# Windowed attention into a two-stage MoE layer: wider score tiles, full-row matmuls, later weight loads, a lagging second stage

## Chip, cores and metric

The kernel runs on one core of a Trainium2 chip. The metric is the device time of one execution in microseconds (us). Three runs of the kernel before took 403.33 to 403.43 us, median 403.37 us. One further execution was recorded by the profiler: 400.38 us, of which the span from the first to the last instruction is 398.7 us. All rows below are from that execution.

## What is computed

Attention with a sliding window of 128 and a linear position bias, on 8 batches, 8 heads, 576 positions, head size 64. Its output, as 4608 tokens of 512, goes through a two-layer network with a gated activation.

```python
scores = q @ k.T / sqrt(64)                       # per batch and head
rel = pos[:, None] - pos[None, :]
bias = -slope[h] * abs(rel)
scores = where((rel >= 0) & (rel < 128), scores + bias, -1e9)
x = softmax(scores) @ v                           # -> (4608, 512)
h = x @ w_in                                      # 512 -> 2048
g = h * sigmoid(beta * h)
out = g @ w_out                                   # 2048 -> 512, float32
```

## The kernel before

**Blocks.** The 576 positions of a batch are four blocks of 128 rows and a fifth of 64. `load_rows` (L84) brings one block of q, k or v for all heads into a float32 buffer of a ring of 14 (`fst`), by a transfer issued on SP. `load_qk` (L95) and `load_v` (L105) cast it to bfloat16 on POOL. SP and POOL each work their queue in order.

**Attention pieces** (each a small group of instructions that TensorE executes as one):
- `T(b, sb)` (L161): eight transposes on TensorE, for four head pairs of q and of k, and one VectorE copy into `qkT`. For the fifth block the transposes are on 64 rows.
- `SC(b, m, p)` (L178): scores of a head pair for two key blocks, 2m and 2m+1. A key block meets the queries of its own block and of the next. The two heads of a pair lie in the lower and upper 64 rows of the array. Four matmuls write the one score buffer in PSUM (`sps`, one buffer). Then four exponentials on ScalarE (L205, L209) and one mask multiply on VectorE (L214) make `pt`. A tile is 512 columns per head for m = 0 and 448 for m = 1.
- `SC4(b)` (L217): the fifth key block of all eight heads by eight 64x64 matmuls, with its own exponential (L229) and multiply by a weight table (L234).
- `PV(b, qb, g)` (L249): for four heads, weights times v, over the previous and own key block, with a column of ones for the sum (L259, L263); then reciprocal and scaling on VectorE (L268, L269). For qb = 4 the weights are 128x64 and 64x64.
- `X(b, qb)` (L274): transposes the result and copies it into `XT`, the input of the first MoE stage (L279, L284).

**MoE pieces**, for nine groups of 512 tokens: `HS(g, j)` (L291) is four matmuls of 512 columns for the j-th 128 columns of w_in, then a tanh on ScalarE (L302) and a combination on VectorE (L303) into `gT` (two buffers). `OS(g, i, n)` (L307) is four of the sixteen matmuls for 128 tokens of the output; after the last, ScalarE copies (L319) and SP stores.

**Order.** TensorE's order is written out by hand (`manual_schedule`): all attention pieces are one list `att`, in which the scores of one half batch are merged with the PVs of the half before. `need[g]` is the number of pieces up to the X that completes the tokens of group g. The pieces up to `need[0]` come first. Then the MoE items of each group follow, HS(g, j) and, from g = 1, OS of the group before alternating with them; between the items the attention pieces for the next group are spread evenly (L405 to L409). The last piece of a group, the X that the next group's first HS reads, comes behind the last item. X of block 3 of batch 0 stands behind T(1,0), T(1,1), T(1,2) and the first SC of batch 1. The orders of the other engines are made by a planner, by program order and its own costs.

**Weights.** W1 (w_in) and W2 (w_out) are loaded by four transfers each, issued on POOL; `issue_after` puts them behind a cast: W1 behind the cast of k of block 3 of batch 0, W2 behind the last cast of v of batch 0 (L383 to L392).

The functions that the change touches:

Of the kernel before, what the change touches and what calls it, by code (L numbers as in the profile page):

```python
# [18 lines left out]
def kernel(  # L19
# [36 lines left out]
    ones = const.tile([P, 2, 512], BF16, name="ones")  # L56
    mask0 = const.tile([P, 2, 512], BF16, name="mask0")
    mask1 = const.tile([P, 2, 448], BF16, name="mask1")
    kpos = const.tile([P, 1], F32, name="kpos")
    bias = const.tile([P, 2, H], F32, name="bias")  # L60
    w4 = const.tile([64, H], F32, name="w4")
    A4 = const.tile([64, 2, NP, 64], F32, name="A4")
    VS = [const.tile([P, NQB, H, D + 2], BF16, name=f"vs{i}") for i in range(2)]
    XT = const.tile([P, NDM, XTR], BF16, name="XT")
# [47 lines left out]
    for sb in range(3):  # L112
        load_qk(0, sb)
# [4 lines left out]
    nc.vector.memset(ones[:], 1.0)  # L118
# [3 lines left out]
    for m, w in ((mask0, P), (mask1, 64)):  # L122
        nc.gpsimd.affine_select(
            out=m[:, :, 0:256], in_=ones[:, :, 0:256], pattern=[[0, 4], [1, P]], **low
        )
        nc.gpsimd.affine_select(
            out=m[:, :, 256 : 256 + w], in_=ones[:, :, 0:w], pattern=[[0, 2], [-1, w]], **up
        )
        nc.gpsimd.affine_select(
            out=m[:, :, 256 + w : 256 + w + P], in_=ones[:, :, 0:P], pattern=[[0, 2], [-1, P]], **up  # L130
        )
# [21 lines left out]
    make_identity(nc, identf[:])  # L153
# [5 lines left out]
    qk_tiles, pts, p4s, xns = {}, {}, {}, {}  # L159

    def T(b, sb):  # L161
        rows = ROWS[sb]
        if sb == 0:
            qk_tiles[b] = qk_pool.tile([P, 2, NP, S], BF16, name="qkT", tag="qkT")
        src = staged.pop((b, sb))
        tps = psum_t.tile([P, 2, NP, P], BF16, name="tps", tag="t")
        for i in range(2):
            for p in range(NP):
                nc.tensor.transpose(  # L169
                    out=tps[:, i, p, 0:rows],  # L170
                    in_=src[0:rows, i, 2 * p : 2 * p + 2, :].rearrange("r h d -> r (h d)"),
                    identity=ident[0:rows, 0:rows],
                )
        nc.vector.tensor_copy(  # L174
            out=qk_tiles[b][:, :, :, P * sb : P * sb + rows], in_=tps[:, :, :, 0:rows]
        )

    def SC(b, m, p):  # L178
        qk = qk_tiles[b]
        sps = psum_s.tile([P, 2, 512], F32, name="sps", tag="sps")  # L180
        w = P if m == 0 else 64
        for kk in range(2):
            kb = 2 * m + kk
            for e in range(2):
                lhsT = qk[64 * e : 64 * e + 64, 1, p, P * kb : P * kb + P]
                if kk == 0:
                    first = sps[:, e, 0:1]
                    o = bass.AP(
                        tensor=first.tensor, offset=first.offset,
                        ap=[list(first.ap[0]), [256 + w, 2], [1, P]],  # L190
                    )
                    nq = 2 * P
                else:
                    o = sps[:, e, P : 2 * P + w]
                    nq = P + w
                nc.tensor.matmul(  # L196
                    o, lhsT=lhsT,
                    rhs=qk[64 * e : 64 * e + 64, 0, p, P * kb : P * kb + nq],
                    start=True, stop=True, skip_group_check=True,
                )  # L200
        wid = 256 + w + P
        pt = pt_pool.tile([P, 2, 512], BF16, name="pt", tag="pt")
        for e in range(2):
            h = 2 * p + e
            nc.scalar.activation(  # L205
                out=pt[:, e, 0:256], in_=sps[:, e, 0:256], func=ACTF.Exp,
                scale=qscale, bias=bias[:, 0, h : h + 1],
            )
            nc.scalar.activation(  # L209
                out=pt[:, e, 256:wid], in_=sps[:, e, 256:wid], func=ACTF.Exp,  # L210
                scale=qscale, bias=bias[:, 1, h : h + 1],
            )
        mk = (mask0 if m == 0 else mask1)[:, :, 0:wid]
        nc.vector.tensor_tensor(out=pt[:, :, 0:wid], in0=pt[:, :, 0:wid], in1=mk, op=ALU.mult)  # L214
        pts[b, m, p] = pt

    def SC4(b):  # L217
        qk = qk_tiles[b]
        sps = psum_s.tile([P, 2, 512], F32, name="sps4", tag="sps")
        for p in range(NP):  # L220
            for e in range(2):
                nc.tensor.matmul(
                    sps[0:64, e, 64 * p : 64 * p + 64],
                    lhsT=qk[64 * e : 64 * e + 64, 1, p, 512:576],
                    rhs=qk[64 * e : 64 * e + 64, 0, p, 512:576],
                    start=True, stop=True, skip_group_check=True,
                )
        e4 = p4_pool.tile([64, 2, NP, 64], F32, name="e4", tag="e4")
        nc.scalar.activation(  # L229
            out=e4[:].rearrange("p e h q -> p e (h q)"), in_=sps[0:64, :, 0:256],  # L230
            func=ACTF.Exp, scale=qscale,
        )
        p4 = p4_pool.tile([64, 2, NP, 64], BF16, name="p4", tag="p4")
        nc.vector.tensor_tensor(out=p4[:], in0=e4[:], in1=A4[:], op=ALU.mult)  # L234
        p4s[b] = p4

    def own(b, kb, h):
        p, e = divmod(h, 2)
        if kb == 4:
            return p4s[b][:, e, p, :]  # L240
        return pts[b, kb // 2, p][:, e, P * (kb % 2) : P * (kb % 2) + P]

    def prev(b, kb, h, nq):
        p, e = divmod(h, 2)
        m, kk = divmod(kb, 2)
        at = 256 if kk else 256 + (P if m == 0 else 64)
        return pts[b, m, p][:, e, at : at + nq]
# [119 lines left out]
    def loads_ahead(b, m):  # L367
# [6 lines left out]
        elif b + 1 < B:  # L374
            for sb in range(3):
                load_qk(b + 1, sb)
            for sb in range(2):
                load_v(b + 1, sb)

    with tc.manual_schedule(engines={mybir.EngineType.PE}):  # L380
        load_v(0, 0)
        load_v(0, 1)
        c = load_qk(0, 3)  # L383
        load_qk(0, 4)
# [12 lines left out]
        for g in range(NTG):  # L397
            items = []
            for j in range(NFF):
                items.append(lambda g=g, j=j: HS(g, j))  # L400
                if g:
                    items.append(lambda g=g, j=j: OS(g - 1, j // 4, j % 4))
            target = need[g + 1] if g + 1 < NTG else len(att)
            start = done
            for n, it in enumerate(items):  # L405
                it()
                while done < start + (target - start) * (n + 1) // len(items):
                    att[done][1]()
                    done += 1  # L409
# [32 lines left out]
```

## Time and profile before

| | before |
|---|---|
| median of 3 runs | 403.37 us |
| profiled execution / its span | 400.38 us / 398.7 us |
| TensorE matmul busy | 354.0 us (89%), 2529 instructions |
| VectorE busy | 231.1 us (58%) |
| ScalarE busy | 214.5 us (54%) |
| POOL busy | 83.2 us (21%) |
| moved by DMA | 42.40 MB, mean 106 GB/s |
| both MoE stages' matmuls | 149.8 + 145.6 us, 576 + 576 of 512 columns |

Busy shares are means over the span. The slices in tenths show stages: in the first fifth the transfers are full and TensorE is not, behind it TensorE is full. Matmuls overlap each other in the records, so the cost of a group of matmuls is read from where it starts to where the next group starts, not from its duration. The engine names are PE (TensorE matmul), PEld (TensorE weight load), DVE (VectorE), ACT (ScalarE), POOL, and SP for the queue that issues transfers.

### The profile page before, as it was taken

To read this page: it belongs to the slowest core of one execution; us is meant where nothing else is said; L and a number is where in the kernel's file an instruction comes from. 1 tells how busy PE (TensorE), PEld (TensorE's weight loads), DVE (VectorE), ACT (ScalarE), POOL (GpSimd) and SP (SyncE) were. 2 spreads that over 40 slices of the span, in tenths; PEclk is the share of its full clock that TensorE was granted. 3 is DMA by queue.
4 is the path that set the end of the run, shared out by engine and by line. 5 is a ranking of instruction groups with operands and counts; after the bars stand their busy time and mean duration, and the time that the engine had idled before them with its cause. 6 is when DMAs were issued, how large, how long until landed. Compare 5 with 4: busy or idle time off the path is not lost.

```text
span 398.7 us, 6725 instructions
## 1 busy us (share of the span) xinstructions
PE 354.0 (89%) x2529; PEld 174.3 (44%) x2529; DVE 231.1 (58%) x485; ACT 214.5 (54%) x446; POOL 83.2 (21%) x143
## 2 busy tenths in 40 slices
PE   0447478889999999999999999999999999999996
PEld 0335224544454445444455445444554444544442
DVE  3556239976675677556665776567666755433410
ACT  1363058666835774475735683568547854345421
POOL 5850255512222312112021312121100000000000
PEclk9955559999999999999999999999999999999999
DMA  9999999941987698834137342000000001000112
GB/s 174 206 198 196 213 198 221 192 108 39 172 189 149 136 199 177 166 89 106 54 84 168 98 115 67 26 29 27 28 26 28 29 26 54 26 27 29 51 53 81
DMA packets 121985, 42.40 MB, mean 106 GB/s; under 512 B 113232, under 2 KB 117344, under 8 KB 121952
## 3 DMA queue, kind: packets, MB, share of 16 engines
q1 hardware_dynamic: 117728, 37.77, 45.4%
q0 software_dynamic: 4224, 4.19, 6.2%
q8 instruction: 20, 0.33, 0.4%
q14 instruction: 13, 0.11, 0.1%
HBM read 36.71 MB, written 9.44 MB: 116 GB/s over the span
## 4 chain that ended last, share of the span: by engine, by line
PE 79%; DMA 9%; DVE 4%; ACT 3%; SPq 2%; issue 1%; POOL 1%; ACTq 0%
PE ops L313 32%; PE hps L297 31%; DMA fst<-in_k_dram 5%; DMA fst<-in_q_dram 4%; PE sps L196 4%; PE pv L263 4%; PE pv L259 3%; PE tps L169 3%; SPq L87 2%; PE xt L279 2%; DVE gT L303 1%; ACT sig L302 1%; DVE XT L284 1%; ACT pt L209 1%; DVE pt L214 1%
## 5 line engine op out<-in xcount | busy, mean ns | idle before, releaser
L302 ACT ACTIVATE sig<-hps,beta_h 128x512 bf16<-128x512 f32 x144 | 99.5, 691 | 116.9 <-PE hps L297 110.6
L297 PE MATMUL hps<-XT,W 128*128 128x512 bf16 x576 | 149.8, 383 | 7.3 <-DVE XT L284 6.6
L313 PE MATMUL ops<-W,gT 128*128 128x512 bf16 x576 | 145.6, 380 | 0.0
L303 DVE SCALAR_TENSOR_TENSOR gT<-sig,hps 128x512 bf16<-128x512 bf16 x144 | 98.5, 684 | 68.4 <-ACT sig L302 68.0
L205 ACT ACTIVATE pt<-sps,bias 128x256 bf16<-128x256 f32 x128 | 61.0, 477 | 44.1 <-PE sps L196 44.0
L297 PEld LDWEIGHTS <-W 128*128 128x128 bf16 x576 | 50.3, 98 | 56.8 <-issue 13.4
L313 PEld LDWEIGHTS <-gT 128*128 128x128 bf16 x576 | 50.6, 98 | 55.7 <-issue 6.0
L209 ACT ACTIVATE pt<-sps,bias 128x192 bf16<-128x192 f32 (+1 forms) x128 | 58.2, 455 | 0.0
L214 DVE TENSOR_TENSOR pt<-pt,mask 128x1024 bf16<-128x1024 bf16 (+1 forms) x64 | 43.7, 683 | 15.4 <-ACT pt L209 14.2
L100 POOL CAST bst<-fst 128x512 bf16<-128x512 f32 (+1 forms) x40 | 24.6, 616 | 117.6 <-issue 72.0
L108 POOL CAST vs<-fst 128x512 bf16<-128x512 f32 (+1 forms) x40 | 26.4, 673 | 67.7 <-PE pv L259 24.3
L196 PE MATMUL sps<-qkT 64*128 64x256 bf16 (+1 forms) x256 | 27.3, 287 | 12.8 <-ACT pt L209 11.2
L269 DVE TENSOR_TENSOR xn<-pv,zs 128x256 bf16<-128x256 f32 (+1 forms) x80 | 33.6, 422 | 2.4
L174 DVE COPY qkT<-tps 128x1024 bf16<-128x1024 bf16 (+1 forms) x40 | 25.4, 635 | 16.2 <-PE tps L169 15.5
L259 PE MATMUL pv<-vs,pt 128*128 128x65 bf16 (+1 forms) x256 | 33.2, 205 | 0.7 <-DVE xn L269 0.6
L169 PE MATMUL tps<-ident,bst 128*128 128x128 bf16 (+1 forms) x320 | 26.0, 230 | 6.8 <-POOL bst L101 4.7
L319 ACT ACTIVATE osb<-ops 128x512 f32<-128x512 f32 x36 | 21.8, 604 | 17.4 <-PE ops L313 16.8
L268 DVE RECIPROCAL zs<-pv 128x4 f32<-128x4 f32 (+1 forms) x80 | 14.3, 179 | 29.0 <-PE pv L263 28.2
L259 PEld LDWEIGHTS <-pt 128*128 128x128 bf16 (+1 forms) x256 | 22.6, 103 | 14.8 <-issue 5.7
L169 PEld LDWEIGHTS <-bst 128*128 128x128 bf16 (+1 forms) x320 | 21.1, 105 | 17.2 <-POOL bst L101 6.1
L101 POOL CAST bst<-fst 128x512 bf16<-128x512 f32 (+1 forms) x40 | 24.5, 611 | 18.0 <-DMA fst<-in_k_dram 18.0
L196 PEld LDWEIGHTS <-qkT 64*128 64x128 bf16 x256 | 9.1, 96 | 37.4 <-issue 35.3
(35 smaller groups left out, 138.5 us busy)
## 6 DMA issues: line engine op xcount, KB each, us to landing
out_dram<-osb SPq DMA_DIRECT2D x36, 256.0 KB, 2.0
fst<-in_q_dram SPq DMA_DIRECT2D x32, 256.0 KB, 4.9
fst<-in_k_dram SPq DMA_DIRECT2D x32, 256.0 KB, 5.1
fst<-in_v_dram SPq DMA_DIRECT2D x32, 256.0 KB, 4.8
W<-in_moe_w_in_dram POOLq DMA_DIRECT2D x4, 512.0 KB, 9.5
W<-in_moe_w_out_dram POOLq DMA_DIRECT2D x4, 512.0 KB, 18.9
fst<-in_q_dram SPq DMA_DIRECT2D x8, 128.0 KB, 4.5
fst<-in_k_dram SPq DMA_DIRECT2D x8, 128.0 KB, 4.3
```

The lines of the kernel that those rows point to most:

```text
L108: return nc.gpsimd.tensor_copy(out=VS[b % 2][0:rows, sb, :, 0:D], in_=f[0:rows])
L169: nc.tensor.transpose(out=tps[:, i, p, 0:rows], in_=src[0:rows, i, 2 * p : 2 * p + 2, :].rearrange("r h d -> r (h d)"), identity=ident[0:r ...
L196: nc.tensor.matmul(o, lhsT=lhsT, rhs=qk[64 * e : 64 * e + 64, 0, p, P * kb : P * kb + nq], start=True, stop=True, skip_group_check=True,)
L205: nc.scalar.activation(out=pt[:, e, 0:256], in_=sps[:, e, 0:256], func=ACTF.Exp, scale=qscale, bias=bias[:, 0, h : h + 1],)
L209: nc.scalar.activation(out=pt[:, e, 256:wid], in_=sps[:, e, 256:wid], func=ACTF.Exp, scale=qscale, bias=bias[:, 1, h : h + 1],)
L214: nc.vector.tensor_tensor(out=pt[:, :, 0:wid], in0=pt[:, :, 0:wid], in1=mk, op=ALU.mult)
L259: nc.tensor.matmul(pv[0:nq, hl, 0 : D + 1], lhsT=prev(b, qb - 1, h, nq), rhs=vs[:, qb - 1, h, 0 : D + 1], start=True, stop=False,)
L269: nc.vector.tensor_tensor(out=xn[0:nq, 4 * g : 4 * g + 4, :], in0=pv[0:nq, :, 0:D], in1=zs[0:nq].broadcast_to([nq, 4, D]), op=ALU.mult,)
L297: nc.tensor.matmul(hps[:], lhsT=W1[:, c, bass.ts(j, P)], rhs=XT[:, c, c0 : c0 + TOKG], start=(c == 0), stop=(c == NDM - 1),)
L302: nc.scalar.activation(out=sig[:], in_=hps[:], func=ACTF.Tanh, scale=beta_h[:, j : j + 1])
L303: nc.vector.scalar_tensor_tensor(out=gts[g][:, j, :], in0=sig[:], scalar=1.0, in1=hps[:], op0=ALU.add, op1=ALU.mult)
L313: nc.tensor.matmul(ops_[:], lhsT=gT[:, j, i * P : i * P + P], rhs=W2[:, j, :], start=(j == 0), stop=(j == NFF - 1),)
```

## The change

- **Score tiles.** The second half of a batch (m = 1) now takes key blocks 2, 4 and 3 in one tile of 512 columns per head; SC4, its weight table and its pools are gone. The fifth block of keys is padded with zeros to 128 rows in `QK`, two fixed tiles in place of the pool `qkT`.
- **Full rows.** PV, T and X of the fifth block work on 128 rows and 128 columns; the extra v rows are zero, and the extra results aren't read.
- **Masks and setup.** The masks are filled from one column of ones by more and smaller selects; identities, masks and biases stand ahead of the first row loads; `fst` has 16 buffers.
- **Weights.** W1 is issued behind the cast of v of block 3 of batch 0, W2 behind the cast of v of block 1 of batch 1.
- **Order.** In group 1 no OS stands beside the first eight HS; two stand behind each of the last eight. In every group the attention pieces are spread over all items but the last three.

```diff
-    fst_pool = ctx.enter_context(tc.tile_pool(name="fst", bufs=14))
+    QK = [const.tile([P, 2, NP, NQB * P], BF16, name=f"qkT{i}") for i in range(2)]
+    fst_pool = ctx.enter_context(tc.tile_pool(name="fst", bufs=16))
...
+    make_identity(nc, identf[:])
+    nc.vector.memset(one[:], 1.0)
...
+    def fill(m, at, n, w, sign, how):
+        for e in range(2):
+            nc.gpsimd.affine_select(
+                out=masks[m][:, e, at : at + n * w].rearrange("p (n w) -> p n w", w=w),
+                in_=bass.AP(tensor=one.tensor, offset=one[:].offset,
+                            ap=[list(one[:].ap[0]), [0, n], [0, w]]),
+                pattern=[[0, n], [sign, w]], **how,
+            )
+    fill(0, 0, 2, P, 1, low)
+    fill(0, 256, 2, P, -1, up)
+    fill(1, 0, 1, P, 1, low)
+    fill(1, 128, 1, 64, 1, low)
+    fill(1, 192, 1, P, 1, low)
+    fill(1, 320, 1, 64, -1, up)
+    fill(1, 384, 1, P, -1, up)
...
+        nc.vector.memset(VS[i][64:P, 4, :, :], 0.0)
+        nc.vector.memset(QK[i][:, :, :, S:], 0.0)
+    for sb in range(3):
+        load_qk(0, sb)
...
     def T(b, sb):
-                    out=tps[:, i, p, 0:rows],
-                    in_=src[0:rows, i, 2 * p : 2 * p + 2, :].rearrange("r h d -> r (h d)"),
-                    identity=ident[0:rows, 0:rows],
+                    out=tps[:, i, p, :],
+                    in_=src[:, i, 2 * p : 2 * p + 2, :].rearrange("r h d -> r (h d)"),
+                    identity=ident[:],
...
+    COLS = {0: (0, 384), 1: (128, 256), 2: (0, 384), 3: (192, 320), 4: (128, None)}
+    OWN = (256, 320)
     def SC(b, m, p):
-        for kk in range(2):
-            kb = 2 * m + kk
+        for kb in ((0, 1), (2, 4, 3))[m]:
+            at, after = COLS[kb]
+            nq = {3: P + 64, 4: 64}.get(kb, 2 * P)
             for e in range(2):
...
+            for half, cols in ((0, slice(0, OWN[m])), (1, slice(OWN[m], 512))):
+                nc.scalar.activation(
+                    out=pt[:, e, cols], in_=sps[:, e, cols], func=ACTF.Exp,
+                    scale=qscale, bias=bias[:, half, h : h + 1],
+                )
+        nc.vector.tensor_tensor(out=pt[:], in0=pt[:], in1=masks[m][:], op=ALU.mult)
-    def SC4(b):
...
+    def weights(b, kb, h, after):
+        p, e = divmod(h, 2)
+        at = COLS[kb][after]
+        return pts[b, min(kb // 2, 1), p][:, e, at : at + P]
     def PV(b, qb, g):
-                    pv[0:nq, hl, 0 : D + 1], lhsT=prev(b, qb - 1, h, nq),
+                    pv[:, hl, 0 : D + 1], lhsT=weights(b, qb - 1, h, 1),
...
-                pv[0:nq, hl, 0 : D + 1], lhsT=own(b, qb, h),
-                rhs=vs[0:nq, qb, h, 0 : D + 1], start=qb == 0, stop=True,
+                pv[:, hl, 0 : D + 1], lhsT=weights(b, qb, h, 0),
+                rhs=vs[:, qb, h, 0 : D + 1], start=qb == 0, stop=True,
     def X(b, qb):
-                out=xt[:, c, 0:nq], in_=xnv[0:nq, c * P : (c + 1) * P], identity=ident[0:nq, 0:nq]
+                out=xt[:, c, :], in_=xnv[:, c * P : (c + 1) * P], identity=ident[:]
...
     def loads_ahead(b, m):
-                load_v(b + 1, sb)
+                c = load_v(b + 1, sb)
+            if b == 0:
+                with tc.issue_after(c.ins):
+                    for n in range(4):
+                        load_w2(n)
...
-        c = load_qk(0, 3)
-        with tc.issue_after(c.ins):
-            for n in range(4):
-                load_w1(n)
         for sb in (2, 3, 4):
             c = load_v(0, sb)
-        with tc.issue_after(c.ins):
-            for n in range(4):
-                load_w2(n)
+            if sb == 3:
+                with tc.issue_after(c.ins):
+                    for n in range(4):
+                        load_w1(n)
...
-                if g:
-                    items.append(lambda g=g, j=j: OS(g - 1, j // 4, j % 4))
+                lag = [2 * j - NFF, 2 * j - NFF + 1] if g == 1 else [j] if g else []
+                items += [lambda g=g, n=n: OS(g - 1, n // 4, n % 4) for n in lag if n >= 0]
-            start = done
+            start, span_ = done, len(items) - 3
...
-                while done < start + (target - start) * (n + 1) // len(items):
+                while done < min(target, start + (target - start) * (n + 1) // span_):
```

## Rows read from the trace of the kernel before

**Rows 1.** The page's 40 slices: TensorE's granted clock and the DMA share, in tenths.
```profile
PEclk9955559999999999999999999999999999999999
DMA  9999999941987698834137342000000001000112
```

**Rows 2.** Busy time by stretch: stretch, its length, busy us (instructions) of each engine.
```profile
62.87:88.28 25.41, 21.29 (x202) 11.37 (x201) 22.17 (x51) 18.68 (x42) 10.19 (x17) 1.00 1.05 180
88.28:380.00 291.72, 287.18 (x2020) 138.01 (x2020) 178.93 (x358) 169.87 (x344) 44.11 (x71) 1.00 0.35 82
```

**Rows 3.** Chain of waits, 10 to 60 us: start us, us, what.
```profile
36.30 13.08 DMA fst<-in_k_dram
...
52.95 1.88 PE hps L297 x4
```

**Rows 4.** The page's DMA queues: packets, MB, share of 16 engines over the span.
```profile
q1 hardware_dynamic: 117728, 37.77, 45.4%
q0 software_dynamic: 4224, 4.19, 6.2%
```

**Rows 5.** Timeline of issues, opening: start us, us, engine, line, what [idle before].
```profile
22.04 2.96 POOL L151 DMA_DIRECT2D W<-in_moe_w_out_dram  x4
...
29.79 6.42 SPq L87 DMA_DIRECT2D fst<-in_q_dram  x1
```

**Rows 6.** Timeline of POOL, its first cast of a row.
```profile
4.33 0.61 POOL L100 CAST bst<-fst 128x512 bf16<-128x512 f32 x1 [2.91 <-DMA fst<-in_q_dram]
```

**Rows 7.** Timeline of TensorE: T(1,4) and the first matmuls of group 1.
```profile
62.87 0.40 PE L169 MATMUL tps<-ident,bst 64*128 64x64 bf16 x8
...
88.28 1.02 PE L297 MATMUL hps<-XT,W 128*128 128x512 bf16 x4 [1.59 <-DVE XT L284]
```

**Rows 8.** Groups of instructions by form: busy us, mean ns of one, idle before.
```profile
L303 DVE SCALAR_TENSOR_TENSOR gT<-sig,hps 128x512 bf16<-128x512 bf16 x144 | 98.5, 684 | 68.4 <-ACT sig L302 68.0
...
L263 PEld LDWEIGHTS <-pt 128*128 128x128 bf16 x256 | 18.5, 102 | 7.9 <-issue 0.4
...
L234 DVE TENSOR_TENSOR p<-e,A 64x512 bf16<-64x512 f32 x8 | 5.6, 704 | 0.3 <-ACT e L229 0.3
```

**Rows 9.** Timeline of TensorE: PV on full rows, then the first of a 64-row PV.
```profile
159.88 1.03 PE L313 MATMUL ops<-W,gT 128*128 128x512 bf16 x4
160.74 0.19 PE L259 MATMUL pv<-vs,pt 128*128 128x65 bf16 x1
...
160.99 1.02 PE L297 MATMUL hps<-XT,W 128*128 128x512 bf16 x4
...
164.91 1.03 PE L313 MATMUL ops<-W,gT 128*128 128x512 bf16 x4
165.86 0.22 PE L259 MATMUL pv<-vs,pt 128*64 128x65 bf16 x1
...
167.03 1.04 PE L297 MATMUL hps<-XT,W 128*128 128x512 bf16 x4
```

**Rows 10.** Timeline of TensorE, 100 to 125 us: score tiles and SC4.
```profile
101.04 0.36 PE L196 MATMUL sps<-qkT 64*128 64x256 bf16 x4
101.34 1.04 PE L297 MATMUL hps<-XT,W 128*128 128x512 bf16 x4
...
103.41 0.37 PE L196 MATMUL sps<-qkT 64*128 64x256 bf16 x4
...
109.00 0.31 PE L222 MATMUL sps<-qkT 64*64 64x64 bf16 x8
109.25 1.04 PE L313 MATMUL ops<-W,gT 128*128 128x512 bf16 x4
...
122.25 0.39 PE L196 MATMUL sps<-qkT 64*128 64x256 bf16 x4
122.57 1.04 PE L313 MATMUL ops<-W,gT 128*128 128x512 bf16 x4
```

**Rows 11.** First-stage matmuls (L297): what TensorE's idle time ended on, us, times.
```profile
  DVE XT L284: 6.6, 9
```

More of the change, by code (lines that the diff above doesn't have):

```diff
@@ L55 @@
     beta_h = const.tile([P, NFF], F32, name="beta_h")
-    ones = const.tile([P, 2, 512], BF16, name="ones")
-    mask0 = const.tile([P, 2, 512], BF16, name="mask0")
-    mask1 = const.tile([P, 2, 448], BF16, name="mask1")
+    one = const.tile([P, 1], BF16, name="one")
+    masks = [const.tile([P, 2, 512], BF16, name=f"mask{m}") for m in range(2)]
     kpos = const.tile([P, 1], F32, name="kpos")
     bias = const.tile([P, 2, H], F32, name="bias")
-    w4 = const.tile([64, H], F32, name="w4")
-    A4 = const.tile([64, 2, NP, 64], F32, name="A4")
     VS = [const.tile([P, NQB, H, D + 2], BF16, name=f"vs{i}") for i in range(2)]
+    QK = [const.tile([P, 2, NP, NQB * P], BF16, name=f"qkT{i}") for i in range(2)]
     XT = const.tile([P, NDM, XTR], BF16, name="XT")
@@ L67 @@
     const.seal()
-    fst_pool = ctx.enter_context(tc.tile_pool(name="fst", bufs=14))
+    fst_pool = ctx.enter_context(tc.tile_pool(name="fst", bufs=16))
     bst_pool = ctx.enter_context(tc.tile_pool(name="bst", bufs=4))
-    qk_pool = ctx.enter_context(tc.tile_pool(name="qk", bufs=2))
     pt_pool = ctx.enter_context(tc.tile_pool(name="ptp", bufs=11))
-    p4_pool = ctx.enter_context(tc.tile_pool(name="p4p", bufs=2))
     xn_pool = ctx.enter_context(tc.tile_pool(name="xn", bufs=2))
@@ L111 @@
     nc.sync.dma_start(out=bflat[:], in_=moe_beta.rearrange("(j p) -> j p", p=P))
-    for sb in range(3):
-        load_qk(0, sb)
+    make_identity(nc, identf[:])
+    nc.vector.memset(one[:], 1.0)
     nc.gpsimd.iota(
@@ L117 @@
     )
-    nc.vector.memset(ones[:], 1.0)
     low = dict(compare_op=ALU.is_ge, fill=0.0, base=0, channel_multiplier=-1)
     up = dict(compare_op=ALU.is_ge, fill=0.0, base=-1, channel_multiplier=1)
[L122 to L131, printed above, removed]
+    def fill(m, at, n, w, sign, how):
[13 more added lines that the diff above has]
+    fill(1, 384, 1, P, -1, up)
     for h in range(H):
@@ L137 @@
             )
-    nc.scalar.activation(out=w4[:], in_=bias[0:64, 0, :], func=ACTF.Exp)
-    for h in range(H):
-        nc.vector.tensor_scalar_mul(A4[:, h % 2, h // 2, :], mask0[0:64, 0, 0:64], w4[:, h : h + 1])
     for i in range(2):
+        nc.vector.memset(VS[i][64:P, 4, :, :], 0.0)
         nc.vector.memset(VS[i][:, :, :, D : D + 1], 1.0)
+        nc.vector.memset(QK[i][:, :, :, S:], 0.0)
+    for sb in range(3):
+        load_qk(0, sb)
     W1v = moe_w_in.rearrange("(c p) f -> p c f", p=P)
@@ L151, in load_w2 @@
         nc.gpsimd.dma_start(out=W2[:, bass.ts(n, 4), :], in_=W2v[:, bass.ts(n, 4), :])
-    make_identity(nc, identf[:])
     bps = psum_t.tile([P, NFF], F32, name="bps", tag="t")
@@ L156 @@
     nc.vector.tensor_scalar_mul(beta_h[:], bps[:], 0.5)
-    qk_tiles, pts, p4s, xns = {}, {}, {}, {}
+    pts, xns = {}, {}
     def T(b, sb):
         rows = ROWS[sb]
-        if sb == 0:
-            qk_tiles[b] = qk_pool.tile([P, 2, NP, S], BF16, name="qkT", tag="qkT")
         src = staged.pop((b, sb))
@@ L169, in T @@
                 nc.tensor.transpose(
-                    out=tps[:, i, p, 0:rows],
-                    in_=src[0:rows, i, 2 * p : 2 * p + 2, :].rearrange("r h d -> r (h d)"),
-                    identity=ident[0:rows, 0:rows],
+                    out=tps[:, i, p, :],
+                    in_=src[:, i, 2 * p : 2 * p + 2, :].rearrange("r h d -> r (h d)"),
+                    identity=ident[:],
                 )
         nc.vector.tensor_copy(
-            out=qk_tiles[b][:, :, :, P * sb : P * sb + rows], in_=tps[:, :, :, 0:rows]
+            out=QK[b % 2][:, :, :, P * sb : P * sb + rows], in_=tps[:, :, :, 0:rows]
         )
+    COLS = {0: (0, 384), 1: (128, 256), 2: (0, 384), 3: (192, 320), 4: (128, None)}
+    OWN = (256, 320)
     def SC(b, m, p):
-        qk = qk_tiles[b]
+        qk = QK[b % 2]
         sps = psum_s.tile([P, 2, 512], F32, name="sps", tag="sps")
-        w = P if m == 0 else 64
-        for kk in range(2):
-            kb = 2 * m + kk
+        for kb in ((0, 1), (2, 4, 3))[m]:
+            at, after = COLS[kb]
+            nq = {3: P + 64, 4: 64}.get(kb, 2 * P)
             for e in range(2):
-                lhsT = qk[64 * e : 64 * e + 64, 1, p, P * kb : P * kb + P]
-                if kk == 0:
-                    first = sps[:, e, 0:1]
+                o = sps[:, e, at : at + min(nq, 512 - at)]
+                if kb in (0, 2):
                     o = bass.AP(
-                        tensor=first.tensor, offset=first.offset,
-                        ap=[list(first.ap[0]), [256 + w, 2], [1, P]],
-                    )
[L192 to L195, printed above, removed]
+                        tensor=o.tensor, offset=o.offset,
+                        ap=[list(o.ap[0]), [after - at, 2], [1, P]],
+                    )
                 nc.tensor.matmul(
-                    o, lhsT=lhsT,
+                    o,
+                    lhsT=qk[64 * e : 64 * e + 64, 1, p, P * kb : P * kb + P],
                     rhs=qk[64 * e : 64 * e + 64, 0, p, P * kb : P * kb + nq],
@@ L200, in SC @@
                 )
-        wid = 256 + w + P
         pt = pt_pool.tile([P, 2, 512], BF16, name="pt", tag="pt")
@@ L204, in SC @@
             h = 2 * p + e
[L205 to L214, printed above, removed]
@@ L215, in SC @@
-        pts[b, m, p] = pt
-    def SC4(b):
[L218 to L235, printed above, removed]
@@ L237, in own @@
-    def own(b, kb, h):
-        p, e = divmod(h, 2)
[L239 to L247, printed above, removed]
+            for half, cols in ((0, slice(0, OWN[m])), (1, slice(OWN[m], 512))):
[3 more added lines that the diff above has]
+                )
@@ L349 @@
             a += [(None, lambda b=b, m=m, p=p: SC(b, m, p)) for p in range(NP)]
-            if m:
-                a.append((None, lambda b=b: SC4(b)))
             att.append((None, lambda b=b, m=m: loads_ahead(b, m)))
@@ L377, in loads_ahead @@
             for sb in range(2):
-                load_v(b + 1, sb)
-    with tc.manual_schedule(engines={mybir.EngineType.PE}):
-        load_v(0, 0)
-        load_v(0, 1)
-        c = load_qk(0, 3)
-        load_qk(0, 4)
-        with tc.issue_after(c.ins):
-            for n in range(4):
-                load_w1(n)
+                c = load_v(b + 1, sb)
[3 more added lines that the diff above has]
+                        load_w2(n)
+    with tc.manual_schedule(engines={mybir.EngineType.PE}):
+        for sb in range(2):
+            load_v(0, sb)
+        for sb in (3, 4):
+            load_qk(0, sb)
         for sb in (2, 3, 4):
             c = load_v(0, sb)
-        with tc.issue_after(c.ins):
-            for n in range(4):
-                load_w2(n)
+            if sb == 3:
+                with tc.issue_after(c.ins):
+                    for n in range(4):
+                        load_w1(n)
         done = 0
```

## Prediction

> **What bounds the kernel now.** I read the slices of the page first. TensorE's clock row and the DMA row [rows 1] split the span in two. Up to about 80 us the transfers are at their limit, and the clock stands at half speed (1.2 GHz) from 20 to 60 us. From there on the DMA share falls and the clock is full (2.4 GHz). Next the busy times by stretch [rows 2]: from 88.28 us, where the second group's first matmul starts, to 380 us TensorE is busy 287.2 of 291.7 us, VectorE 178.9, ScalarE 169.9. So behind 88 us every microsecond taken from TensorE's order is a microsecond of time. Between 62.87 and 88.28 us TensorE has 21.3 and VectorE 22.2 busy of 25.4 us: two engines near their limit, neither at it. Before that the chain of waits [rows 3] runs through row transfers, the last a row of k from 36.30 to 49.38 us, and the first matmul of the first MoE group, HS(0,0), starts at 52.95 us.
>
> So there are three accounts: the opening up to T(1,4) at 62.87 us, the rest of group 0, and the steady part.
>
> **The opening: weight loads.** A full row tile is 256 KB. The queue summary [rows 4] gives the rows and outputs 45.4% of 398.7 us for 37.77 MB, so a row costs 181.0 / 37.77 x 0.262 = 1.26 us of all 16 engines; the eight weight transfers take 6.2%, 24.7 us, so 12.4 us for W1 and 12.4 for W2. W2 is issued from 22.04 us on, W1 just ahead of it; while they run, the row queue issues one row per 6.42 us [rows 5]. In those 6.42 us the weights get 6.42 - 1.26 = 5.2 us.
>
> HS(0,0) needs X(0,3), which stands in TensorE's order behind T(1,2) and SC(1,0,0), so it needs six rows of batch 1. Today both weights run ahead of them. In the changed order only W1 does. Bytes up to k(1,2): 12 full and 3 half rows of batch 0 plus 6, that is 19.5 x 1.26 = 24.5 us, plus W1 12.4, plus 3.1 us until transfers run (an estimate: the first cast at 4.33 us [rows 6], less one row) = 40.0 us. The same sum with W2 gives 52.4 against 49.38 in the trace, so up to 3 come off: 37 to 40 us. From there the trace needs 52.95 - 49.38 = 3.6 us to HS(0,0): about 42 us, 11 earlier.
>
> That isn't all kept. W2 now waits for the cast of v(1,1), two rows later, about 42 us, and floods the queue there. Its four issues (2.96 us together on POOL) stand ahead of the casts of batch 1's blocks 3 and 4, whose rows land later anyway. Rows still to come for T(1,4): 0.8 of k(1,3) and two half rows, 1.8 x 6.42 = 11.6 us from a flood start at 43: T(1,4) about 55 us. TensorE has from HS(0,0) to T(1,4) 62.87 - 52.95 = 9.9 us of work [rows 3, 7], some 11 at half clock throughout, so it comes there at 53 to 54 and waits a little. T(1,4) moves from 62.87 to 55: 7.9 us. Bounds: 0 (all bytes ahead of T(1,4), W2 among them, are the same in both orders) and 11 (HS(0,0)'s whole lead). I take 7.
>
> Setup edits (fourteen mask selects in place of six, memsets, an earlier identf, row casts behind the masks) cost nothing: POOL idles 2.91 us before the first cast [rows 6], and TensorE waits for rows of 37 us and later. Without that cover, at most 5 us on POOL. Two more fst buffers let two more rows be asked for; the engines are full in that stretch: 0.
>
> **The rest of group 0** (62.87 to 88.28 us). Removed are the 1.59 us wait ahead of HS(1,0) [rows 7], since the attention items now end three items early; two slow PV blocks (1.0 us each, below); SC4 (0.34, below): 4.9 us of TensorE. But VectorE keeps 22.2 us less SC4's multiply of 0.70 [rows 8], with four mask multiplies a seventh wider: about 21.7. So the stretch can't fall below about 22, and I take 25.4 - 22.4 = 3 us (bounds 0 and 3.7). What is late next here is VectorE.
>
> **The steady part** (batches 2 to 7, and the starts of groups 2 to 8).
> PV of the 64-row block: eight matmuls that alternate 128x64 and 64x64. They start 0.146 us apart and take 165.86 to 167.03 = 1.17 us; the four MoE matmuls before them take 0.95 (164.91 to 165.86) instead of 0.86 (159.88 to 160.74), so 0.09 to enter. The eight full-row ones take 160.74 to 160.99 = 0.25 with nothing to enter [rows 9]. The change makes the first kind into the second: 1.17 + 0.09 - 0.25 = 1.0 us, twice a batch: 2.0.
> SC4: 109.00 to 109.25 = 0.25, plus 0.09 to enter [rows 10]: 0.34 gone.
> SC of the second half: today 101.04 to 101.34 = 0.30 for 448 columns of each head, the first half 122.25 to 122.57 = 0.32 for 512 [rows 10]. After: 512 columns and two more matmuls. Columns 0.02; two matmuls between 0.02 and 0.16 (a quarter of 0.32 each). I take 0.06 in all, four a batch: 0.24 lost.
> The 64-row transposes (T and X of block 4) lose their entry of 0.09 each and stream as many or twice the columns: between -0.1 and +0.1, taken as 0.
> Sum 2.0 + 0.34 - 0.24 = 2.1 us a batch, 6 batches: 12.6 us.
> Waits for XT at group starts: nine, 6.6 us in all [rows 11]; less HS(0,0)'s 0.52 and HS(1,0)'s 1.59 [rows 3, 7] leaves 4.5 for seven. The last X is now three items (2.6 us) ahead, and the wait is some 0.5 us long: all go. What is late next is ScalarE's chain behind the single score buffer, a rival below.
> Second stage of group 0 moved into the second half of group 1: TensorE's sum is unchanged, but eight HS items run with only seven attention items between them. HS costs 0.86 on TensorE and 0.68 on VectorE [rows 8], so TensorE stays first or level; I take 1 us lost (bounds 0 and 4). gT has two buffers, and group 2 writes the freed one after group 1 as before. The first output stores move back as far; on SP they then stand behind the rows of batch 3's first blocks.
>
> **Sum**: 7 + 3 + 12.6 + 4.5 - 1 = 26 us. The profiled execution took 400.38 us (span 398.7), so 374 there; the median of the runs is 403.37, 3 us above it, and 403.37 - 26 = 377.
>
> **Rivals.**
> (a) The opening gives nothing: the flood of W2 holds k(1,4) until T(1,4) is where it was. For: the bytes are the same, and 6.42 us a row is steep. Against: four HS and three score tiles go ahead of it. 377 + 7 = 384.
> (b) ScalarE paces the score tiles. One buffer: the next SC waits for four exponentials of the last. With slow PV blocks gone, items are denser. Against: two MoE items with one score tile and a PV take 2.37 (101.04 to 103.41 [rows 10]) with no idle time noted ahead of the second tile. If 0.15 us is lost at each of 56 tiles: 8 us, 385.
> (c) The weight loads of the full-row PV blocks are not hidden. A load is 102 ns [rows 8]; eight would make the block 0.25 + 0.82 = 1.07 us, the saving 0.2 a block, 12 x 0.8 = 9.6 us less: 387. Against: loads of that size belong to the block of rows 9 too, whose matmuls start 0.03 us apart. The Trainium skill has it otherwise: TensorE: Matmul & The Clock Gate, Part 3 (The mechanism), says that a weight load runs beside a matmul in flight only if their row groups differ, which full-row matmuls never do. By that rule (c) would hold; rows 9 disagree with it, since 0.03 us leaves no room for a load in line.
> (d) Slower: the clock. TensorE's work from 42 us on is broken by the waits for T(1,3) and T(1,4), and the half-speed stage, which today ends at 60 us, 7 us behind the first HS [rows 1], goes on through group 1. At half clock each microsecond elapsed loses half of one; the 26 us are eaten if it lasts 52 us beyond 55, to 107 us. To 115 us it gives 407. Against: from T(1,4) on TensorE's work is as dense as that which ended the stage today.
> (e) The planned order on POOL puts the weights elsewhere than the text suggests; then the opening and the lag give nothing or cost: 385 to 387.
>
> **How the numbers follow.** Forecast 0.58 (own range 371 to 382), (a) 0.18, (b) 0.11, (c) 0.03, (d) 0.05, (e) 0.05. Bounds: all the upper ends (11, 3.7, 13.6, 4.5, 0) make 33 us, 370; the opening at 0, the lag at 4 and half of (b) make 391. I state 369 to 389. 0.2% is 0.8 us, what a measurement here can tell from no change. Only (d) is slower, 0.05; within 0.2% needs several misses at once, 0.02; faster 0.93.
>
> **What would show it.** HS(0,0) near 42 us and T(1,4) near 55; HS(1,0) near 78; no XT wait over 0.1 us behind group 1; PV of block 4 in 0.25 us; score tiles of the second half 0.31 to 0.40 us; TensorE busy some 13 us less from group 1 on. It is wrong if T(1,4) stays at 62, if TensorE gets waits on ScalarE ahead of score tiles, or if the clock row shows half speed behind 65 us.

## The result, and the profile after

The changed kernel takes 375.51 us (median of 4 runs, 373.84 to 377.03) against 403.35 us before: ratio 0.9319, 95% interval 0.9267 to 0.9372. A second set of runs on one chip, the base of the first experiments, gave 374.47 us and 0.9295 (0.9281 to 0.9309). The forecast was 377.

The profiled execution took 376.31 us, span 374.6. Against 398.7 before that is 24.1 us less, where the medians differ by 27.8; the recorded execution of before was 3 us under its median, that of after 0.8 above its own. The account below goes by the two traces.

First the page of the changed kernel: busy times, then from the 40 slices TensorE's clock and the DMA share.

```profile
PE 338.5 (90%) x2529; PEld 172.7 (46%) x2529; DVE 224.2 (60%) x473; ACT 214.4 (57%) x437; POOL 84.4 (23%) x151
...
PEclk9999999899999999999999999999999999999999
DMA  9999999999297898954138440000000010001012
```

TensorE is 15.5 us less busy. The transfers are full for ten slices, to 94 us, where before they were full for eight, to 80 us [rows 1]; the bytes are the same 42.40 MB. The clock row shows 9 but for one 8, where before it had 5 from 20 to 60 us; more on that below. The two stretches that answer to [rows 2], T(1,4) to the first HS of group 1, and from there on:

```profile
52.46:81.05 28.59, 21.03 (x201) 12.31 (x200) 22.89 (x49) 18.10 (x40) 12.58 (x20) 0.94 1.11 204
...
81.05:356.00 274.95, 272.65 (x2022) 135.87 (x2021) 175.43 (x352) 170.65 (x339) 43.47 (x72) 1.00 0.40 91
```

The marks in TensorE's timeline that answer to [rows 3, 7]: HS(0,0), T(1,4), the tenth HS of group 0, the pair of HS(0,15) and HS(1,0), one HS of group 1.

```profile
42.44 1.87 PE L267 MATMUL hps<-XT,W 128*128 128x512 bf16 x4 [0.52 <-DVE XT L254]
...
52.46 0.61 PE L171 MATMUL tps<-ident,bst 128*128 128x128 bf16 x8
...
68.53 1.91 PE L267 MATMUL hps<-XT,W 128*128 128x512 bf16 x4
...
80.19 1.89 PE L267 MATMUL hps<-XT,W 128*128 128x512 bf16 x8 [0.73 <-DVE gT L273]
...
87.30 1.02 PE L267 MATMUL hps<-XT,W 128*128 128x512 bf16 x4 [1.04 <-DVE gT L273]
```

HS(1,0) is the second four of the eight from 80.19: 80.19 + 0.86 = 81.05 us. The last run of OS matmuls begins at 380.19 us in the chain of before and at 356.12 in that of after, and takes 14.69 us in both. So the 24.1 us split as follows:

| stretch | before | after | gain | predicted |
|---|---|---|---|---|
| to T(1,4) | 62.87 | 52.46 | 10.4 | 7 |
| T(1,4) to HS(1,0) | 25.41 | 28.59 | -3.2 | 3 |
| HS(1,0) to the last OS run | 291.91 | 275.07 | 16.8 | 16.1 |

The transfers and casts on POOL, to set beside [rows 5]:

```profile
20.46 3.14 POOL L153 DMA_DIRECT2D W<-in_moe_w_in_dram  x4
...
38.92 0.61 POOL L97 CAST bst<-fst 128x512 bf16<-128x512 f32 x1 [3.78 <-DMA fst<-in_k_dram]
...
41.64 2.97 POOL L156 DMA_DIRECT2D W<-in_moe_w_out_dram  x4
...
46.23 0.64 POOL L97 CAST bst<-fst 64x512 bf16<-64x512 f32 x1
...
55.97 0.61 POOL L104 CAST vs<-fst 128x512 bf16<-128x512 f32 x1 [6.95 <-DMA fst<-in_v_dram]
```

W1 goes out at 20.46 us, k(1,2) is cast at 38.92, W2 goes out at 41.64. The four rows for T(1,3) and T(1,4) were already under way by then and are cast by 46.87; the flood of W2 falls on v(1,3), which POOL awaits for 6.95 us, and that row isn't needed yet.

Last, all PV matmuls are now of one form, which answers to [rows 8, 9], and the waits ahead of HS (what TensorE's idle time ended on, us, times) answer to [rows 11]:

```profile
L233 PE MATMUL pv<-vs,pt 128*128 128x65 bf16 x320 | 31.0, 200 | 2.5 <-DVE xn L239 1.5 <-DVE pt L211 0.9
```

One block of eight in the steady part, its first two matmuls and what follows the eighth (0.24 us in all):

```profile
160.86 0.19 PE L229 MATMUL pv<-vs,pt 128*128 128x65 bf16 x1
160.89 0.20 PE L233 MATMUL pv<-vs,pt 128*128 128x65 bf16 x1
...
161.10 1.03 PE L283 MATMUL ops<-W,gT 128*128 128x512 bf16 x4
```

The waits:

```profile
  DVE gT L273: 3.0, 5
  DVE XT L254: 0.5, 1
```

The eight XT waits at group starts are gone; only HS(0,0)'s is left. The five waits on gT (0.5 us in all before) run from HS(0,15), 0.73 us, into the first half of group 1, 2.3 us. Score tiles of the second half, beside [rows 10]:

```profile
94.67 0.40 PE L197 MATMUL sps<-qkT 64*128 64x256 bf16 x6
94.99 1.04 PE L283 MATMUL ops<-W,gT 128*128 128x512 bf16 x4
...
99.47 0.40 PE L197 MATMUL sps<-qkT 64*128 64x256 bf16 x6
99.80 1.04 PE L267 MATMUL hps<-XT,W 128*128 128x512 bf16 x4
```

A tile takes 0.32 to 0.33 us in place of 0.30: 64 more columns and two more matmuls for 0.03.

### The profile page after: what moved, and what is told of

Read it like the earlier page. It is cut to its first block, busy times and chain, and to the rows that moved or that the text cites. A ratio compares the mean times of both kernels' runs of the same rounds, so it can differ in the third digit from the quotient of the medians.

```text
span 374.6 us, 6713 instructions
## 1 busy us (share of the span) xinstructions
PE 338.5 (90%) x2529; PEld 172.7 (46%) x2529; DVE 224.2 (60%) x473; ACT 214.4 (57%) x437; POOL 84.4 (23%) x151
## 2 busy tenths in 40 slices
DMA packets 121985, 42.40 MB, mean 113 GB/s; under 512 B 113232, under 2 KB 117344, under 8 KB 121952
## 4 chain that ended last, share of the span: by engine, by line
PE 80%; DMA 6%; DVE 4%; ACT 4%; SPq 4%; issue 1%; POOL 0%; ACTq 0%
PE ops L283 34%; PE hps L267 32%; PE sps L197 4%; DMA fst<-in_k_dram 4%; PE tps L171 4%; SPq L83 4%; ACT pt L207 3%; PE xt L249 2%; PE pv L233 2%; DVE gT L273 2%; PE pv L229 2%; DMA fst<-in_v_dram 1%; ACT sig L272 1%; DVE pt L211 1%; DVE qkT L176 1%
## 5 line engine op out<-in xcount | busy, mean ns | idle before, releaser
L207 ACT ACTIVATE pt<-sps,bias 128x256 bf16<-128x256 f32 (+2 forms) x256 | 100.4, 480 | 34.9 <-PE sps L197 34.6
L267 PEld LDWEIGHTS <-W 128*128 128x128 bf16 x576 | 51.1, 98 | 56.5 <-issue 10.9
L211 DVE TENSOR_TENSOR pt<-pt,mask 128x1024 bf16<-128x1024 bf16 x64 | 46.1, 720 | 21.2 <-ACT pt L207 20.0
L197 PE MATMUL sps<-qkT 64*128 64x256 bf16 (+2 forms) x320 | 28.3, 271 | 14.1 <-ACT pt L207 13.1
L171 PE MATMUL tps<-ident,bst 128*128 128x128 bf16 x320 | 28.8, 240 | 7.8 <-POOL bst L96 4.3
L233 PE MATMUL pv<-vs,pt 128*128 128x65 bf16 x320 | 31.0, 200 | 2.5 <-DVE xn L239 1.5
L171 PEld LDWEIGHTS <-bst 128*128 128x128 bf16 x320 | 23.5, 107 | 17.3 <-POOL bst L96 4.9
L197 PEld LDWEIGHTS <-qkT 64*128 64x128 bf16 x320 | 12.4, 97 | 38.2 <-issue 35.1
L233 PEld LDWEIGHTS <-pt 128*128 128x128 bf16 x320 | 23.6, 102 | 13.7 <-issue 1.8
L229 PE MATMUL pv<-vs,pt 128*128 128x65 bf16 x256 | 25.8, 200 | 1.8 <-DVE qkT L176 1.2
L229 PEld LDWEIGHTS <-pt 128*128 128x128 bf16 x256 | 21.3, 102 | 8.3 <-DVE xn L239 1.3
## 6 DMA issues: line engine op xcount, KB each, us to landing
W<-in_moe_w_out_dram POOLq DMA_DIRECT2D x4, 512.0 KB, 12.6
```

Of the source, the lines that this page charges most:

```text
L171: nc.tensor.transpose(out=tps[:, i, p, :], in_=src[:, i, 2 * p : 2 * p + 2, :].rearrange("r h d -> r (h d)"), identity=ident[:],)
L197: nc.tensor.matmul(o, lhsT=qk[64 * e : 64 * e + 64, 1, p, P * kb : P * kb + P], rhs=qk[64 * e : 64 * e + 64, 0, p, P * kb : P * kb + nq], ...
L207: nc.scalar.activation(out=pt[:, e, cols], in_=sps[:, e, cols], func=ACTF.Exp, scale=qscale, bias=bias[:, half, h : h + 1],)
L211: nc.vector.tensor_tensor(out=pt[:], in0=pt[:], in1=masks[m][:], op=ALU.mult)
L229: nc.tensor.matmul(pv[:, hl, 0 : D + 1], lhsT=weights(b, qb - 1, h, 1), rhs=vs[:, qb - 1, h, 0 : D + 1], start=True, stop=False,)
L233: nc.tensor.matmul(pv[:, hl, 0 : D + 1], lhsT=weights(b, qb, h, 0), rhs=vs[:, qb, h, 0 : D + 1], start=qb == 0, stop=True,)
```

## The experiments

Ratios are to the kernel before, run beside each on the same chip. The first set has the changed kernel as its base; the two later sets ran on other chips without it, and are compared with that base through the kernel before, which took 403.1 to 403.25 us on all three.

> The changed kernel once more, as the base for the three beside it. Every theory: 374 to 377 us, ratio to the kernel before 0.93.

374.47 us, ratio 0.9295 (0.9281 to 0.9309). In its trace a late transpose of batch 2, HS(0,9) and the pair with HS(1,0) stand here:

```profile
65.53 0.61 PE L171 MATMUL tps<-ident,bst 128*128 128x128 bf16 x8 [0.92 <-POOL bst L96]
65.97 1.03 PE L267 MATMUL hps<-XT,W 128*128 128x512 bf16 x4
...
76.91 1.89 PE L267 MATMUL hps<-XT,W 128*128 128x512 bf16 x8 [1.11 <-DVE gT L273]
```

The span is 371.3 us, 3.3 less than in the first trace: 0.9 of it is there by HS(0,0) (41.56 us against 42.44), 1.9 by T(1,4) (50.55 against 52.46), all by HS(1,0) (77.8 against 81.05). In the first trace HS(0,0) and HS(0,9) took 1.87 and 1.91 us, the pace of the half-speed stage; here they took 1.02 and 1.03. So the two traces differ at least in part by how much of the opening and of group 0 runs at half speed. That the other runs spread for this reason is not shown.

**PV of the 64-row block put back.**

```diff
-                    pv[:, hl, 0 : D + 1], lhsT=weights(b, qb - 1, h, 1),
+                    pv[0:nq, hl, 0 : D + 1], lhsT=weights(b, qb - 1, h, 1)[:, 0:nq],
...
-                pv[:, hl, 0 : D + 1], lhsT=weights(b, qb, h, 0),
-                rhs=vs[:, qb, h, 0 : D + 1], ...
+                pv[0:nq, hl, 0 : D + 1], lhsT=weights(b, qb, h, 0)[0:nq, 0:nq],
+                rhs=vs[0:nq, qb, h, 0 : D + 1], ...
```

> The changed kernel with the PV of the 64-row block alone put back to 128x64 and 64x64 matmuls that alternate. Theory (the alternating shapes cost 1.17 + 0.09 us a block against 0.25, and TensorE is the bound behind 90 us): 12 blocks x 1.0 = 12 us, and 0 to 2 us for the two blocks of batch 1, so 387 to 390 us. Rival (the block lay beside other work, and the gain came from the weights and the order): under 3 us more, 376 to 378.

389.77 us, ratio 0.9665 (0.9645 to 0.9685): 15.3 us slower than its base. One block in its trace:

```profile
160.97 1.03 PE L283 MATMUL ops<-W,gT 128*128 128x512 bf16 x4
161.93 0.22 PE L229 MATMUL pv<-vs,pt 128*64 128x65 bf16 x1
162.08 0.21 PE L233 MATMUL pv<-vs,pt 64*64 64x65 bf16 x1
...
163.10 1.04 PE L267 MATMUL hps<-XT,W 128*128 128x512 bf16 x4
```

161.93 to 163.10 is 1.17 us again. From HS(1,0) to the last OS run this trace takes 12.3 us more than the changed kernel's, the 12 blocks of the theory. The rest, 3 us by the medians where 0 to 2 were expected, lies ahead of it: the matmuls of batch 0's two blocks start 0.19 us apart, and with them HS(0,0) comes at 43.60 us. This one edit is over half of the whole gain, and the theory stands.

**The same block, but all 128x64:** as above, with `lhsT=weights(b, qb, h, 0)[:, 0:nq]` and `rhs=vs[:, ...]` for the second matmul too.

> As the run with the 64-row PV block put back, but its matmuls all of one shape, 128x64, so that shapes don't alternate within the block. Theory (each change between array shapes costs, about 0.1 us): one change to enter and one to leave, matmuls 0.03 to 0.06 us apart within: 0.25 to 0.5 us a block, 3 to 6 us over the changed kernel, 377 to 381. Rival (weights of 64 columns are slow by themselves, at 0.146 us a matmul): as with the alternating shapes, about 390 us.

377.51 us, ratio 0.9362 (0.9337 to 0.9386), 0.7% above its base by the ratios.

```profile
154.14 1.03 PE L283 MATMUL ops<-W,gT 128*128 128x512 bf16 x4
155.10 0.22 PE L229 MATMUL pv<-vs,pt 128*64 128x65 bf16 x1
155.15 0.20 PE L233 MATMUL pv<-vs,pt 128*64 128x65 bf16 x1
155.19 0.19 PE L229 MATMUL pv<-vs,pt 128*64 128x65 bf16 x1
...
155.34 0.19 PE L233 MATMUL pv<-vs,pt 128*64 128x65 bf16 x1
155.47 1.04 PE L267 MATMUL hps<-XT,W 128*128 128x512 bf16 x4
```

The start is late by 0.1 us, then the matmuls start 0.03 to 0.05 us apart, and the block takes 0.37 us. Weights of 64 columns aren't slow, nor are 64x64 matmuls by themselves: SC4's eight took 0.25 us [rows 10]. The change of shape is: eight alternating matmuls cost 1.17 us, eight alike 0.37. The Trainium skill, TensorEngine Tiling (Array Packing), Key Properties, says that a change of the tiling mode, as opposed to the tile, drains TensorE; these two runs agree in that a change costs time, and give it a price of about 0.1 us.

**No lag in group 1:** `lag = [j] if g else []`.

> The changed kernel with OS of group 0 beside each HS of group 1 from the start, as before. Theory (with no OS between them the HS of group 1 run into the two hps buffers, which the trace of the changed kernel shows as 3.0 us of waits on gT): these waits go, 2 to 3 us less, 372.5 to 373.5 us. Rival 1 (W2 lands so late that OS(0,0) must wait, which is what the lag is for): 2 us or more slower, with a wait of OS on a transfer. Rival 2 (attention in group 1 is spread anew and pays it back): no change within 0.8 us.

372.14 us, ratio 0.9223 (0.9197 to 0.9249): 2.3 us faster than its base. The waits ahead of HS in its trace:

```profile
  DVE gT L273: 0.9, 1
  DVE XT L254: 0.5, 1
```

Four of the five gT waits are gone; the one left is ahead of HS(0,15). No OS waits for W2. The theory stands: the lag costs.

**Attention spread over all items again:** `span_ = len(items)`.

> The changed kernel with the attention pieces spread over all items again, not all but the last three. Theory (the wait of the first HS of a group for XT comes back, 8 times, 0.5 us and more each): 4.5 us in groups 2 to 8 and 1.6 ahead of group 1, less up to 3 us, since attention is less dense in group 0: 378 to 381 us. Rival (the gap is hidden, or the denser pieces cost as much as the wait): 375 to 376.

375.94 us, ratio 0.9319 (0.9304 to 0.9334): 1.5 us slower, less than the theory said, and inside the rival's range.

```profile
  DVE XT L254: 5.1, 9
  DVE gT L273: 2.0, 3
```

The waits are back in full, 4.6 us more. But its HS(1,0) stands at 75.82 us against 77.8 in the base: group 0 ends 2 us earlier when its attention pieces aren't crowded into 13 of 16 items (from T(1,4) on it takes 24.8 us, against 27.2 in the base). So neither side had it whole: the gap is not hidden, as the theory said, and the denser pieces cost part of what the waits do, as the rival said. The two traces are 3.3 us apart, the medians 1.5; the difference is in which execution was recorded, the base's fastest and this one's slowest.

**Weights as before, in the changed kernel:** W1 behind `load_qk(0, 3)`, W2 behind the last `load_v(0, sb)`.

> The changed kernel with both weights issued where they were before (W1 behind the cast of k of block 3, W2 behind the last v of batch 0). Theory (the weights ahead of batch 1's rows set the start of the first MoE group): HS(0,0) back at 50 to 53 us, and 6 to 9 us slower in all: 381 to 384 us. Rival (what group 0 starts earlier it loses to dense attention behind it, on VectorE and ScalarE): HS(0,0) back at 52, but group 1 starts within 3 us of where it does now: 375 to 378.

385.71 us, ratio 0.9565 (0.9543 to 0.9586): 11.2 us above the base of the first set. HS(0,0) is back at 53.08 us, HS(1,0) at 89.31 + 0.86 = 90.2, 9 to 12 us later than in the two traces of the changed kernel. The theory stands, its size was low: the whole lead is kept.

**The new places of the weights, in the kernel before:** the same edit the other way round.

> The kernel before with nothing but the new places of the weight loads. Theory: HS(0,0) at 42 to 43 us in place of 53, T(1,4) about 52 to 55, and from there on as before: 6 to 9 us faster, 394 to 397. Rival (the flood of W2 moves to the rows that group 0 needs): 0 to 3 us faster, 400 to 403.

397.03 us, ratio 0.9853 (0.9834 to 0.9873): 6.1 us faster, within the theory's figure. But HS(0,0) came at 46.7, not 42 to 43. Pieces of its chain of waits:

```profile
30.39 0.47 ACT pt L205
31.90 0.57 PE sps L196 x4
32.50 0.47 ACT pt L205
34.43 0.56 PE xt L279 x4
...
42.66 1.84 PE tps L169 x16
...
46.72 0.59 PE hps L297
```

No row transfer stands in this part: the score tiles of batch 0, one after the other through the single buffer, and TensorE's own order set the time. In that order stand batch 0's two slow PV blocks, whose sixteen matmuls start 0.19 us apart between 38.64 and 42.66 us. Its k(1,2) was cast at 38.81 us, as early as in the changed kernel.

**Setup in the old order** (row loads of batch 0 ahead of masks; identf behind them).

> The changed kernel with the order of setup as before: row loads of batch 0 first, masks and identf among and behind their casts. The prediction's step (setup costs and brings nothing, since TensorE waits for rows of 37 us and later): HS(0,0) stays at 42, 374 to 376 us. Rival (with the weights moved, batch 0's own chain of scores is as late as the rows: in the run with the weights alone moved HS(0,0) came at 46.7 us, 7 us behind its last row): T(0,0) starts at 11 to 12 us in place of 6, HS(0,0) 2 to 3 us later, 376 to 378 us.

378.37 us, ratio 0.9380 (0.9348 to 0.9411): 3 to 4 us slower than the changed kernel. The rival had it. POOL's cast of k(1,2), and HS(0,0):

```profile
39.19 0.61 POOL L97 CAST bst<-fst 128x512 bf16<-128x512 f32 x1 [0.31 <-DMA fst<-in_k_dram]
```

```profile
45.84 1.86 PE L267 MATMUL hps<-XT,W 128*128 128x512 bf16 x4 [0.52 <-DVE XT L254]
```

The row is there as before, HS(0,0) comes 3.4 us later. So "setup is covered" was true of the kernel before alone; once the rows come at 39 us, batch 0's chain, which the old setup starts late, is the later of the two. What starts it late shows at the head of TensorE's order, the small transpose of moe_beta, here and then in the changed kernel:

```profile
13.09 0.28 PE L159 MATMUL bps<-identf,bflat 16*128 16x16 f32 x1 [13.09 <-POOL identf masks.py:199]
```

```profile
2.58 0.25 PE L159 MATMUL bps<-identf,bflat 16*128 16x16 f32 x1 [2.58 <-DMA bflat<-in_moe_beta_dram]
```

It waits for `identf`, which POOL makes behind the masks, and T(0,0) stands behind it: 13.31 us, against 5.94 in the changed kernel. The casts wait for the masks too (k of block 2 at 12.98 us against 10.72). The first score tile starts at 16.07 us in place of 11.93; how much of this is `identf` alone was not separated.

**T and X of the 64-row block on 64 rows**, as before the change.

> The changed kernel with the transposes T and X of the 64-row block back on 64 rows. The prediction's step (they lose 0.09 us of entry and stream more columns, 0 taken, between -0.1 and +0.1 each): 374 to 376 us, no change within 0.8 us. Rival (the change of array shape costs more than its 0.09 on entry, on leaving too): 2 to 3 us slower, 377 to 378 us.

376.62 us, ratio 0.9341 (0.9314 to 0.9368), against 0.9319 (0.9267 to 0.9372) and 0.9295 (0.9281 to 0.9309) for the changed kernel. Not told apart from it by the first interval; by the second some 0.6 to 3 us slower. The traces say more: from HS(1,0) to the last OS run this one takes 275.6 us, the changed kernel's two 275.1 each, so the edit costs 0.5 us there, where TensorE is full. That is nearer to the step's 0 than to the rival's 2; what it costs in the opening stays open.

**Fourteen row buffers:** `bufs=14`.

> The changed kernel with 14 row buffers in place of 16. The prediction's step (the engines are full, more rows asked for bring nothing): no change, 374 to 376 us. Rival (two rows fewer are in flight when a weight flood starts, so T(1,3) or T(1,4) waits for a flooded row): T(1,4) later than 52.5 us, 1 to 3 us slower.

375.25 us, ratio 0.9312 (0.9285 to 0.9339): no change, as the step said. T(1,4) came at 52.99 us, 0.5 later than the rival's mark, but the four rows it needs were not what it waited for, and the time did not move.

**A better version: no lag, and early attention only from group 1 on.**

```diff
-                lag = [2 * j - NFF, 2 * j - NFF + 1] if g == 1 else [j] if g else []
+                lag = [j] if g else []
-            start, span_ = done, len(items) - 3
+            start, span_ = done, len(items) - (3 if g else 0)
```

> A version meant to beat the changed kernel: no lag in group 1, and attention pieces early by three items only from group 1 on, not in group 0. Theory (group 0 is bound by VectorE and ScalarE, and its last three HS without attention leave TensorE to the hps buffers; the one XT wait of 1.6 us ahead of group 1 comes back): 372.1 as without the lag, less 1 to 3 us: 369 to 371. Rival (the XT wait eats it): 372 to 373.

368.35 us (368.24 to 368.97), ratio 0.9143 (0.9126 to 0.9159): the fastest, and a little below the expected range. HS(1,0) in its trace pays the XT wait and is still some 1.5 to 5 us earlier than in the two traces of the changed kernel:

```profile
76.27 1.02 PE L267 MATMUL hps<-XT,W 128*128 128x512 bf16 x4 [0.94 <-DVE XT L254]
```

**And with the weights later still:** only the first quarter of W1 behind v(0,3), the rest behind v(1,1), W2 behind v(1,4).

> A version meant to beat all: no lag, attention early by three items only from group 1 on, and weights later still: only the first quarter of W1 behind v of block 3 of batch 0, the other three behind v of block 1 of batch 1, W2 behind the last v of batch 1. Theory (rows before HS(0,0) set its time, and each quarter of W1 holds them 3.1 us): k(1,2) lands 9 us earlier, but batch 0's own chain then binds at about 39 us, so HS(0,0) 2 to 4 us earlier: 365 to 367 us. Rival 1 (HS of quarters two to four, or OS(0,0), waits for its weights): 368 or more. Rival 2 (group 0 is bound by VectorE and ScalarE whatever its start): 368.

370.0 us, ratio 0.9177 (0.9154 to 0.92), where 365 to 367 was expected: no faster than the last, by the ratios 0 to 0.8% slower. The cast of k(1,2) and HS(0,0):

```profile
31.35 0.62 POOL L97 CAST bst<-fst 128x512 bf16<-128x512 f32 x1
```

```profile
42.32 1.86 PE L267 MATMUL hps<-XT,W 128*128 128x512 bf16 x4 [0.52 <-DVE XT L254]
```

The row came 7.6 us earlier and HS(0,0) not at all: batch 0's chain holds it at 42. Rows and chain meet there in the changed kernel.

## Why the prediction was right

The time came within 1.5 us of the forecast, and the main terms (the weights' lead to HS(0,0), the slow PV blocks, the XT waits) were right. That it came so close is partly luck: in the traces the first step gave 3.4 us more than forecast and the second 6.2 less. In the repeated trace they gave 12.3 and -1.8 us, so the border between them moves by some 2 us.

**HS(0,0) near 42:** 42.44. The sum by bytes was right, and the weights are worth their whole lead (11.2 us undone, 6.1 alone). It left something out: setup, costed at nothing, is what lets the chain of batch 0 be there at 42. The cover named for it, rows of 37 us and later, is too short in the very kernel that was forecast: with the old setup the chain of batch 0 ends behind the row. That term was 3 to 4 us of the gain, hidden in the figure for HS(0,0). The same chain holds batch 0's two PV blocks, which the sum left out: slow, they put HS(0,0) at 43.60.

**T(1,4):** 52.46 where 55 was said, the term 10.4 where 7 was taken (bounds 0 and 11). The step that failed is "rows still to come for T(1,4): 0.8 of k(1,3) and two half rows" in the flood. All four were under way when W2 was issued and were cast by 46.87; the flood hit v rows with time to spare. (In the repeated trace it reached further: a transpose of batch 2 waited 0.92 us for a row issued behind them.) TensorE's own order, with a wait of 1.70 us for ScalarE in it, set T(1,4), as it would by the 9.9 us of [rows 3, 7].

**The rest of group 0:** 3.2 us lost where 3 were to be gained, outside the bounds of 0 and 3.7. VectorE has 22.9 us of work where about 21.7 was said. The step that failed is that this floor was taken for the time: no engine is full, and the chain of waits of this stretch is 9.6 us on ScalarE, 9.4 on VectorE and 7.3 on TensorE. Part of it is the attention crowded into 13 items: the even spread gives 2 us back, and still takes 24.8 us where 22.4 was said. (The 4.9 us said to be taken from TensorE are 3.9 by their own terms, 1.59 + 2.0 + 0.34; the forecast did not use them.) And of rival (d) this much came true in this trace: HS(0,9) at 68.53 us, behind the 65 us named, took 1.91 us in place of 1.03, in a slice where the clock row dips to 8. It passed by HS(0,10), and was not the stage of 50 us that the rival needed.

**The steady part:** 16.8 against 12.6 + 4.5 - 1 = 16.1. Three terms were undone alone: PV of the 64-row block (12.3 us here, 15.3 with the blocks ahead of it), the XT waits (6.6 to 0.5, of which 4.5 here), the lag (2.3 us of gT waits where 1 was taken, and 2.3 us by the run without it). SC4's 2.0 us and the score tiles, 0.03 dearer instead of 0.06, are read from rows, no run undid them. With the 0.5 us of T and X these make 12.3 + 2.0 + 4.5 + 0.5 - 0.7 - 2.3 = 16.3; the last 0.5 us is open. Rival (c) fell: eight full-row matmuls still start 0.03 us apart. Rival (b) didn't come: from 92 to 330 us TensorE is busy 237.75 of 238 us, so nothing waits on ScalarE there.

## What to carry to other kernels

Read the cost of a small block from where it starts to where the next starts, and compare blocks of one shape with blocks that alternate: padding 64 rows to 128 took out 15 us here though it adds arithmetic. A cover ("this waits for rows anyway") has to be checked in the kernel after the other edits, not before. And work that fills an engine's gaps shouldn't be taken away from a stretch with shallow buffers, even when the sum stays the same.

## What was not expected of the hardware

- A change of array shape between neighbouring matmuls costs about 0.1 us: 1.17 us for eight that alternate, 0.37 for eight of 128x64, 0.25 for eight of 128x128 [rows 9] and for eight of 64x64 [rows 10].
- The clock row can miss the half-speed stage: in the changed kernel it shows 9 at 42 us, and the four HS matmuls there took 1.87 us, as the four at 52.95 us before, where it showed 5, half speed (1.2 GHz) [rows 1, 3]. At full speed (2.4 GHz) four take 1.03 in the same records. The pace of a known matmul is the surer sign.
